# Context rows of V from DRAM, GpSimd interleaving and running sums in a chunked-attention and feed-forward kernel

## The chip, the cores and the metric

One core of a Trainium2 chip runs the whole program. The metric is device microseconds of one execution. TensorE is called PE in the profile, VectorE DVE, ScalarE ACT, GpSimd POOL and SyncE SP. The last two also issue DMAs: GpSimd those that convert float32 to float16 on the way (loads of q, k, v and the weights), SyncE all others, the DMA transposes among them.

## The reference, cut to what matters

```python
# q, k, v: (4, 8, 768, 64); mem_k, mem_v: (4, 8, 8, 64)
chunk, left_ctx, right_ctx = (32, 16, 8)
for c in range(24):
    ...
    k_ctx = k[:, :, l_start:r_end]          # 16 before, the chunk, 8 after
    v_ctx = v[:, :, l_start:r_end]
    k_full = np.concatenate([mem_k, k_ctx], axis=2)
    v_full = np.concatenate([mem_v, v_ctx], axis=2)
    a = softmax(scale * q_c @ k_full.T)
    out[:, :, c_start:c_end] = a @ v_full
# heads side by side: x is (4, 768, 512)
mu, var = x.mean(-1), ((x - mu) ** 2).mean(-1)
xn = (x - mu) / np.sqrt(var + 1e-06) * g_ln
result = x + np.maximum(xn @ w_ch1, 0.0) @ w_ch2     # 512 -> 2048 -> 512
```

## The kernel before, in words

The 4 x 768 rows are 24 tiles of 128 rows, six to a batch. A tile holds four chunks, which are worked in two groups of two chunks, so a batch has 12 groups of 64 rows. A group has 96 columns of keys and 96 rows of values: 8 memory rows, 16 rows from the left, 64 of its own, 8 from the right. In `V` (two buffers, by batch) a group's values stand on 96 partitions: memory on 0 to 7, left context on 8 to 23, its own rows on 24 to 87, right context on 88 to 95. In `KT` (two buffers) the keys stand transposed, 96 columns for each group and pair of heads.

Attention of a tile is `scores` (16 small matmuls), two `soften` (exponentials on ScalarE), `values` (16 small matmuls; column 64 of each head gives the sum for the softmax), then a reciprocal and a multiplication on VectorE, which leave x in float32 in `xs`. `stats` gives mean and variance on VectorE, `norm` writes (x - mean) * g to `xn`, and `root` makes the reciprocal of the deviation on GpSimd (`veps`, `rstd`); it is applied at the very end, in `finish`. `turn_x` transposes xn to `xT`, by TensorE for the first six tiles and by a DMA transpose on SyncE's queue for the others.

The feed-forward part works on units of three tiles, eight units, `u` from 0 to 7. Each unit has 28 steps: 16 `up` steps (four matmuls of 384 columns, then a relu, on VectorE for even steps and on ScalarE for odd ones) and 12 `down` steps (four matmuls of 512 columns; the last of each tile is followed by `finish` on VectorE and a store). `up_tile` does one chunk of four hidden blocks for a single tile. PSUM gives the ups and downs four banks (`mm0` to `mm3`) and attention two double banks (`att`).

The order is written by hand: `at(u, step, ...)` puts a piece of other work behind a step, `attend` places a tile's attention in this way, and every engine does its share in the order of the program. Step s of unit u is written (u, s) here. Ahead of unit 0 stands a front, in which the first three tiles are worked while weights arrive; there, TensorE also does dummy matmuls (`warm`).

Keys and queries of batch 0 are turned by TensorE (`turn_tile`). For batches 1 to 3, `load_block` loads a block of 256 rows, in two DMAs; `mix` interleaves it on ScalarE from `st` into `iv`; `cross` transposes it by DMA on SyncE's queue into `rawk` (keys) or `QR` (queries); and `spread` copies `rawk` into `KT` in three copies on VectorE, with `key_left` and `key_right` for the context between tiles. `load_v` loads values. Its default covers a group's own 64 rows, and `v_left` and `v_right` then copy the context from neighbouring groups, between partitions, by DMAs on SyncE's queue (V<-V in the profile); for the first groups of batch 0 the loads already bring some context rows. `v_mem` copies the memory values into V.

## Time and profile before

| what | us |
|---|---|
| median of 3 runs (lowest, highest) | 292.23 (290.86, 293.84) |
| profiled execution, its own time | 292.26 |
| its span, first to last instruction | 290.5 |
| TensorE busy | 228.5 (79%) |
| VectorE, GpSimd, ScalarE busy | 148.4, 120.5, 87.6 |
| mean granted clock of TensorE | 0.894 of full speed |

The span is what the trace covers; the rest of an execution lies around it. Shares of busy time are means over stages with different limits.

### The profile page before, as it was taken

Reading aid. Unit: us, or ns where it says so; the run is one execution under the profiler, and the core shown is the slowest. Engines: PE = TensorE matmul, PEld = TensorE weight load, DVE = VectorE, ACT = ScalarE, POOL = GpSimd, SP = SyncE. Lnnn points to the kernel's source line nnn. Section 1 sums busy time; section 2 is a strip of 40 time slices with the busy share of each in tenths; the row PEclk is TensorE's granted clock in tenths of the full one; section 3 lists DMA queues with packets and bytes.
Section 4 is the critical chain, followed back from the end, with each engine's and each line's share of the span. In section 5 each row is a group of like instructions: output and inputs, shape, how many; then the busy total and the mean of one; then the engine's idle time right before and its main releaser. Section 6 shows DMA issues by size and latency. Waiting matters only on the chain.

```text
span 290.5 us, 5094 instructions
## 1 busy us (share of the span) xinstructions
PE 228.5 (79%) x2024; PEld 132.9 (46%) x2024; DVE 148.4 (51%) x306; ACT 87.6 (30%) x148; POOL 120.5 (41%) x173
## 2 busy tenths in 40 slices
PE   7575899747095859996092999999086999999994
PEld 3353654446072325652051555654043646645644
DVE  5475543825314653726563463737574853863412
ACT  2424224133244103732240321642123603510400
POOL 8872630499920218656900119474930130110000
PEclk9979799997777868999589699999658999999999
DMA  6999990288999345999964024999946122012012
GB/s 109 165 184 208 196 140 2 72 125 93 139 130 93 90 80 67 158 86 147 164 128 67 18 56 77 157 102 138 182 93 101 20 66 82 18 54 93 0 38 72
DMA packets 87096, 29.12 MB, mean 100 GB/s; under 512 B 74872, under 2 KB 83344, under 8 KB 87024
## 3 DMA queue, kind: packets, MB, share of 16 engines
q0 software_dynamic: 53632, 13.86, 50.9%
q1 hardware_dynamic: 33440, 14.94, 29.5%
q8 instruction: 16, 0.26, 0.4%
q14 instruction: 8, 0.07, 0.1%
HBM read 27.95 MB, written 6.29 MB: 118 GB/s over the span
## 4 chain that ended last, share of the span: by engine, by line
PE 48%; DMA 26%; DVE 9%; POOL 6%; issue 4%; SPq 3%; ACT 2%; DVEq 0%; ACTq 0%; POOLq 0%
PE mm L335 20%; PE mm L361 19%; DMA V<-V 7%; DMA rawk<-iv 5%; DMA QR<-iv 4%; DMA out_dram<-osb 3%; DVE KT L100 3%; DMA st<-in_q_dram 3%; PE att L251 2%; PE att L272 2%; POOL st L123 2%; DMA st<-in_k_dram 2%; SPq L228 2%; DMA xT<-xn 2%; POOL V L100 2%
## 5 line engine op out<-in xcount | busy, mean ns | idle before, releaser
L335 PE MATMUL mm<-xT,w1c 128*128 128x384 f16 (+1 forms) x496 | 93.6, 345 | 20.4 <-DMA xT<-xn 17.1
L361 PE MATMUL mm<-w2c,rT 128*128 128x512 f16 x368 | 88.2, 394 | 0.0
L335 PEld LDWEIGHTS <-w1c 128*128 128x128 f16 x496 | 56.0, 118 | 48.9 <-issue 29.7
L327 ACT ACTIVATE rT<-mm 128x384 f16<-128x384 f32 (+2 forms) x66 | 31.8, 484 | 109.6 <-DVE rT L329 51.7
L300 POOL TENSOR_SCALAR veps<-mv 128x1 f32<-128x1 f32 x24 | 10.1, 423 | 116.2 <-DVE mv L290 115.9
L329 DVE TENSOR_SCALAR rT<-mm 128x384 f16<-128x384 f32 (+2 forms) x65 | 35.3, 545 | 39.1 <-PE mm L335 36.1
L361 PEld LDWEIGHTS <-rT 128*128 128x128 f16 x368 | 35.5, 101 | 41.9 <-issue 5.3
L261 ACT ACTIVATE AT<-att,band 96x512 f16<-96x512 f32 x48 | 31.1, 679 | 23.9 <-PE att L251 23.7
L100 DVE COPY KT<-rawk 128x288 f16<-128x288 f16 (+2 forms) x27 | 22.7, 894 | 28.5 <-DMA rawk<-iv 28.5
L130 POOL DMA_DIRECT2D V<-in_v_dram x48 | 34.8, 730 | 5.0 <-DMA V<-in_v_dram 2.8
L370 DVE SCALAR_TENSOR_TENSOR osb<-mm,rstd,xs 128x512 f32<-128x512 f32 x23 | 17.0, 746 | 26.8 <-PE mm L361 25.2
L98 ACT COPY iv<-st 128x1024 f16<-128x1024 f16 x18 | 18.6, 1042 | 38.0 <-DMA rawk<-iv 22.3
L272 PE MATMUL att<-V,AT 96*64 96x65 f16 x384 | 11.9, 208 | 19.5 <-DMA V<-V 17.3
L272 PEld LDWEIGHTS <-AT 96*64 96x64 f16 x384 | 9.3, 119 | 27.4 <-issue 18.9
L100 POOL COPY V<-memv 8x2560 f16<-8x2560 f16 x9 | 21.5, 2413 | 0.0
L294 DVE SCALAR_TENSOR_TENSOR xn<-xs,mv,gb 128x512 f16<-128x512 f32 x24 | 17.9, 747 | 0.5
L279 DVE RECIPROCAL rec<-att 128x8 f32<-128x8 f32 x24 | 4.9, 203 | 24.1 <-PE att L272 24.0
L280 DVE TENSOR_TENSOR xs<-att,rec 128x512 f32<-128x512 f32 x24 | 16.6, 691 | 0.8
L289 DVE BATCH_NORM_STATS2 bst<-xs 128x6 f32<-128x512 f32 x24 | 16.6, 693 | 0.7
L346 PE MATMUL mm<-xT,w1c 128*128 128x128 f16 x112 | 10.0, 260 | 8.3 <-ACT rT L327 7.2
L251 PE MATMUL att<-QR,KT 64*96 64x64 f16 x384 | 14.2, 216 | 1.5 <-DVE KT L100 1.2
L251 PEld LDWEIGHTS <-KT 64*96 64x96 f16 x384 | 11.5, 129 | 8.3 <-issue 5.7
(55 smaller groups left out, 129.5 us busy)
## 6 DMA issues: line engine op xcount, KB each, us to landing
out_dram<-osb SPq DMA_DIRECT2D x23, 256.0 KB, 2.7
st<-in_k_dram POOLq DMA_DIRECT2D x24, 128.0 KB, 7.4
st<-in_q_dram POOLq DMA_DIRECT2D x24, 128.0 KB, 8.1
V<-in_v_dram POOLq DMA_DIRECT2D x40, 64.0 KB, 8.3
w1c<-in_moe_w_ch_dram POOLq DMA_DIRECT2D x4, 512.0 KB, 8.9
w2c<-in_moe_w_ch_dram POOLq DMA_DIRECT2D x4, 512.0 KB, 10.5
V<-in_v_dram POOLq DMA_DIRECT2D x5, 88.0 KB, 7.9
V<-V SPq DMA_DIRECT2D x2, 220.0 KB
```

The lines of the kernel that those rows point to most:

```text
L98: eng.copy(out=out, in_=in_)
L100: eng.tensor_copy(out=out, in_=in_)
L130: nc.gpsimd.dma_start(out=V[b % 2][lo:hi, g, :, 0:64], in_=dram(v, b * H * HS + (64 * g - 24 + lo) * D, [[64, hi - lo], [HS, H], [1, 64]]),)
L251: nc.tensor.matmul(out=p[0:W, par, (4 * gg + j) * 64 : (4 * gg + j) * 64 + 64], lhsT=KT[b % 2][rows, t, j, gg, :], rhs=free(QR[b % 2][rows ...
L261: nc.scalar.activation(out=free(AT[t % 3], 32 * c, [[64, 16], [1, 32]]), in_=free(p, 4 * c, [[64, 16], [1, 4], [8, 8]], W), func=ACTF.Exp, ...
L272: nc.tensor.matmul(out=p[64 * gg : 64 * gg + 64, par, HD * j : HD * j + HD], lhsT=AT[t % 3][:, par, gg, j, :], rhs=V[b % 2][:, 2 * t + gg, ...
L294: nc.vector.scalar_tensor_tensor(out=xn[i % 4], in0=xs[i % 9], scalar=mv[t][:, 0:1], in1=gb, op0=ALU.subtract, op1=ALU.mult,)
L327: nc.scalar.activation(out=o, in_=p, func=ACTF.Relu)
L329: nc.vector.tensor_scalar(out=o, in0=p, scalar1=0.0, scalar2=None, op0=ALU.max)
L335: nc.tensor.matmul(out=p, lhsT=free(w1c[c][:, dt, :], i, [[4, 128]]), rhs=xT[u % 2][:, dt, 128 * lo : 128 * (lo + n)], start=(dt == 0), st ...
L361: nc.tensor.matmul(out=p, lhsT=rT[c][:, k_, 128 * i : 128 * i + 128], rhs=w2c[c][:, k_, :], start=(c == 0 and k_ == 0), stop=(c == 3 and k ...
L370: nc.vector.scalar_tensor_tensor(out=o, in0=p, scalar=rstd[t % 9], in1=xs[t % 9], op0=ALU.mult, op1=ALU.add,)
```

## The change

- `load_v` now loads each group's context rows from DRAM as well (88 rows; 72 and 80 at a batch's ends), for all batches. `v_left` and `v_right` are gone.
- `mix` runs on GpSimd, and `iv` has four buffers instead of two. The loads, mixes and memory copies of a batch are one list, `ahead`; the transposes (`cross`) of a batch are placed at fixed steps.
- In `spread`, two of the three copies go to ScalarE. `KT` is laid out by group.
- `root` of all tiles of a unit stands in that unit's own steps 3 to 5 (12 for one tile, 16 to 18 in unit 0), not behind the tile's attention.
- The sum over x comes from the multiplication that writes it (`accum_out`), the mean is that sum times -1/512 (`nmean`), and the sum of squared deviations (`sq`) is a Square on ScalarE with its accumulator.
- In the front, the loads, the attention of three tiles and six `up_tile` are ordered anew; unit 0 starts at up step 8 instead of 4. The load of g is issued later.

```diff
-    def load_v(b, g, lo=24, hi=88):
+    def load_v(b, g):
+        lo, hi = 24 if g == 0 else 8, 88 if g == NG - 1 else 96
...
-    def v_left(b, g0, g1):
...
-    def spread(b, blk, eng):
+    def spread(b, blk, eng, e1):
-        copy(eng, free(kt, 768 * t + 24, [[192, 4], [8, 9], [1, 8]]),
+        copy(e1, free(kt, 768 * t + 24, [[96, 4], [8, 9], [1, 8]]),
...
-        nc.vector.tensor_tensor(
-            out=x.rearrange("p (a h d) -> p a h d", a=2, h=4),
...
+        nc.vector.scalar_tensor_tensor(
+            out=x.rearrange("p (h d) -> p h d", h=8),
+            in0=free(p, 0, [[128, 8], [1, 64]]), scalar=1.0,
+            in1=free(r, 0, [[1, 8], [0, 64]]),
+            op0=ALU.mult, op1=ALU.mult, accum_out=tot[t],
+        )
+        nc.vector.tensor_scalar(
+            out=nmean[t], in0=tot[t], scalar1=-1.0 / 512, scalar2=None, op0=ALU.mult
+        )
...
-        nc.vector.bn_stats(out=bst[t % 3], in_=x)
-        nc.vector.bn_aggr(out=mv[t], in_=bst[t % 3])
+        nc.scalar.activation(
+            out=junk, in_=xs[(NT * b + t) % 9], func=ACTF.Square, bias=nmean[t], scale=1.0,
+            accum_out=sq[t],
+        )
...
-        at(u, s1 + 2, root, b, t)
-        at(u, s1 + 3, turn_x, b, t)
+        at(u, s1 + 1, norm, b, t)
+        at(u, s1 + 2, turn_x, b, t)
+        at(u, s1 + 2, stats, b, t)
+        at(i // 3, 12 if i == 5 else 3 + i % 3, root, b, t)
...
+        order = [(load_pair, (0,)), (load_pair, (1,))]
+        order += [(mem_cols, (pool,)), (v_mem, (0, 4, pool)), (mix_pair, (0,))]
+        order += [(load_v, (g,)) for g in range(3)]
+        order += [(mix_pair, (1,)), (v_mem, (4, 8, pool))]
...
+            ahead(1, order, 23, 0.3)
+            for blk, s in ((0, 1), (1, 4), (2, 14)):
...
+                at(1, s + 4, spread, 1, blk, dve, act)
+            attend(6, 11, 14, 1)
+            attend(7, 14, 18, 1)
+            attend(8, 18, 22, 1)
...
+            ahead(b, order, U * (u - 1), 1)
+            for blk, s in ((0, 7), (1, 12), (2, 24)):
```

GpSimd's queue behind the last loads of batch 0, in the kernel before (a name's number tells buffers apart; `st` and `V` are loads of batch 1, `mv` the statistics of a tile):

```order
L300 TENSOR_SCALAR veps_133<-mv_130 128x1
L304 TENSOR_TENSOR rstd_139<-veps_133,mhalf 128x1
L300 TENSOR_SCALAR veps_134<-mv_131 128x1
L304 TENSOR_TENSOR rstd_140<-veps_134,mhalf 128x1
L123 DMA st_87<-in_k_dram 128x1x512 x2
L123 DMA st_88<-in_q_dram 128x1x512 x2
L100 COPY KT_96<-memKT 128x24x8 x2
L100 COPY V_94<-memv_67 8x2560
L123 DMA st_81<-in_k_dram 128x1x512 x2
```

The same place in the changed kernel, from the root of the front's last tile on:

```order
L296 TENSOR_SCALAR veps_147<-sq_140 128x1
L300 TENSOR_TENSOR rstd_150<-veps_147,mhalf 128x1
L125 DMA st_87<-in_k_dram 128x1x512 x2
L125 DMA st_88<-in_q_dram 128x1x512 x2
L125 DMA st_81<-in_k_dram 128x1x512 x2
L125 DMA st_82<-in_q_dram 128x1x512 x2
L102 COPY KT_98<-memKT 128x48x8
L102 COPY V_96<-memv_67 8x2560
L102 COPY iv_89<-st_87 128x2x8x64
L102 COPY iv_90<-st_88 128x2x8x64
L133 DMA V_96<-in_v_dram 72x8x64
```

The roots of tiles 3 and 4 no longer stand ahead of the loads of batch 1, and the interleaves (`iv`) now stand in this queue.

SyncE's queue from the last output of unit 0 on, before:

```order
L373 DMA out_dram<-osb_123 128x512
L137 DMA V_93<-V_93 16x1280
L141 DMA V_93<-V_93 8x640
L228 DMA_TRANSPOSE rawk_91<-iv_89 128x8x128
L228 DMA_TRANSPOSE QR_98<-iv_90 128x8x128
L228 DMA_TRANSPOSE rawk_92<-iv_89 128x8x128
L228 DMA_TRANSPOSE QR_98<-iv_90 128x8x128
L137 DMA V_94<-V_94 16x3200
L141 DMA V_94<-V_94 8x3200
```

And now:

```order
L369 DMA out_dram<-osb_125 128x512
L221 DMA_TRANSPOSE rawk_93<-iv_89 128x8x128
L221 DMA_TRANSPOSE QR_100<-iv_90 128x8x128
L221 DMA_TRANSPOSE rawk_94<-iv_91 128x8x128
L221 DMA_TRANSPOSE QR_100<-iv_92 128x8x128
L221 DMA_TRANSPOSE rawk_93<-iv_89 128x8x128
L221 DMA_TRANSPOSE QR_100<-iv_90 128x8x128
L308 DMA_TRANSPOSE xT_117<-xn_115 128x4x128
```

The copies between partitions are gone, and the transposes of batch 1 follow one another, each from a buffer of its own up to the fourth.

VectorE in the first steps of unit 1, from the values of tile 5 on, before:

```order
L279 RECIPROCAL rec_146<-att_147 128x8
L280 TENSOR_TENSOR xs_107<-att_147,rec_146 128x512
L289 BN_STATS bst_126<-xs_107 128x6
L290 BN_AGGR mv_132<-bst_126 128x2
L329 TENSOR_SCALAR rT_119<-mm_152 128x256
L294 SCALAR_TENSOR_TENSOR xn_112<-xs_107,mv_132,gb 128x512
L322 COPY xT_116<-att_148 128x4x128
L329 TENSOR_SCALAR rT_119<-mm_150 128x256
L329 TENSOR_SCALAR rT_120<-mm_152 128x256
L329 TENSOR_SCALAR rT_117<-mm_149 128x4x128
L100 COPY KT_96<-rawk_91 128x4x72
```

And now:

```order
L272 RECIPROCAL rec_158<-att_160 128x8
L273 SCALAR_TENSOR_TENSOR xs_109,tot_131<-att_159,rec_158 128x512
L279 TENSOR_SCALAR nmean_137<-tot_131 128x1
L102 COPY KT_98<-rawk_93 128x8x88
L325 TENSOR_SCALAR rT_120<-mm_161 128x256
L285 SCALAR_TENSOR_TENSOR xn_114<-xs_109,nmean_137,gb 128x512
L318 COPY xT_118<-att_159 128x4x128
L325 TENSOR_SCALAR rT_121<-mm_163 128x256
```

The first spread copy of batch 1 moved up, ahead of the norm of tile 5.

## Rows read from the trace of the kernel before

**Rows 1.** The page: busy time of each engine, share of the span, instructions.

```profile
PE 228.5 (79%) x2024; PEld 132.9 (46%) x2024; DVE 148.4 (51%) x306; ACT 87.6 (30%) x148; POOL 120.5 (41%) x173
```

**Rows 2.** Waits of TensorE (PE), whole span: total us, times, longest us.

```profile
PE att L272 <- DMA V<-V: 17.3, 5, 4.8
PE mm L335 <- DMA xT<-xn: 17.1, 2, 9.3
...
PE mm L346 <- ACT rT L327: 7.2, 1, 7.2
```

**Rows 3.** Timeline of TensorE: start, us, instruction, idle time before it.

```profile
31.19 4.51 PE L335 MATMUL mm<-xT,w1c 128*128 128x384 f16 x24
36.91 4.06 PE L335 MATMUL mm<-xT,w1c 128*128 128x384 f16 x24 [1.21 <-DVE rT L329]
40.81 1.03 PE L361 MATMUL mm<-w2c,rT 128*128 128x512 f16 x4
...
57.88 1.47 PE L335 MATMUL mm<-xT,w1c 128*128 128x256 f16 x12 [0.22 <-DVE xT L322]
...
71.69 1.06 PE L346 MATMUL mm<-xT,w1c 128*128 128x128 f16 x16
...
127.79 7.94 PE L361 MATMUL mm<-w2c,rT 128*128 128x512 f16 x36
```

**Rows 4.** Windows: us, busy PE, PEld, DVE, ACT, POOL; clock, DMA share, GB/s.

```profile
80.40:100.90 20.50, 17.58 (x169) 10.45 (x168) 8.48 (x19) 7.33 (x12) 3.00 (x6) 0.76 0.97 106
111.60:135.70 24.10, 24.10 (x209) 13.58 (x207) 14.28 (x28) 10.41 (x17) 14.68 (x24) 1.00 1.60 117
265.80:290.50 24.70, 20.99 (x129) 13.39 (x127) 7.59 (x13) 3.93 (x8) 0.00 (x0) 1.00 0.12 43
```

**Rows 5.** Timeline of GpSimd (POOL): first loads of batch 1; copies of batch 2.

```profile
38.49 0.55 POOL L304 TENSOR_TENSOR rstd<-veps,mhalf 128x1 f32<-128x1 f32 x1
...
55.61 0.19 POOL L300 TENSOR_SCALAR veps<-mv 128x1 f32<-128x1 f32 x1 [3.15 <-DVE mv L290]
...
56.37 1.59 POOL L123 DMA_DIRECT2D st<-in_k_dram  x2
...
138.58 7.01 POOL L100 COPY V<-memv 8x2560 f16<-8x2560 f16 x3
```

**Rows 6.** Groups by line and form: count, busy us, mean ns, idle before.

```profile
L289 DVE BATCH_NORM_STATS2 bst<-xs 128x6 f32<-128x512 f32 x24 | 16.6, 693 | 0.7
...
L290 DVE BATCH_NORM_AGGREGATE mv<-bst 128x2 f32<-128x6 f32 x24 | 4.4, 182 | 0.8
...
L294 DVE SCALAR_TENSOR_TENSOR xn<-xs,mv,gb 128x512 f16<-128x512 f32 x24 | 17.9, 747 | 0.5
...
L100 POOL COPY V<-memv 8x2560 f16<-8x2560 f16 x9 | 21.5, 2413 | 0.0
...
L100 POOL COPY KT<-memKT 128x192 f16<-128x192 f16 x6 | 1.9, 352 | 0.0
...
L98 ACT COPY iv<-st 128x1024 f16<-128x1024 f16 x18 | 18.6, 1042 | 38.0 <-DMA rawk<-iv 22.3 <-DMA QR<-iv 13.8 <-DMA st<-in_k_dram 2.0
```

**Rows 7.** DMA queue in 175:205: packets, MB, share of 16 engines.

```profile
q0 software_dynamic: 11087, 2.18, 93.5%
```

**Rows 8.** Timeline of SyncE (SP): two key transposes of batch 1.

```profile
69.55 1.34 SPq L228 DMA_TRANSPOSE rawk<-iv  x1
...
77.07 2.37 SPq L228 DMA_TRANSPOSE rawk<-iv  x1
```

**Rows 9.** Timeline of VectorE (DVE): spread copies that waited for transposes.

```profile
75.92 1.50 DVE L100 COPY KT<-rawk 128x288 f16<-128x288 f16 x3 [2.38 <-DMA rawk<-iv]
...
86.90 1.41 DVE L100 COPY KT<-rawk 128x288 f16<-128x288 f16 x3 [2.02 <-DMA rawk<-iv]
...
141.07 5.52 DVE L100 COPY KT<-rawk 128x288 f16<-128x288 f16 x3 [5.81 <-DMA rawk<-iv]
```

**Rows 10.** DMA issues, whole span: count, median us to landing.

```profile
rawk<-iv SPq DMA_TRANSPOSE x9, 3.1
```

More of the change, by code (lines that the diff above doesn't have):

```diff
@@ L447 @@
     nc.vector.memset(V[0][64:96, NG - 1, :, :], 0.0)
[L448 to L449 removed]
     load_tile(0, 1, 1)
+    load_v(0, 0)
+    load_v(0, 1)
     load_tile(0, 2, 0)
     load_w1(0)
[L453 to L454 removed]
+    load_v(0, 2)
+    load_v(0, 3)
     load_tile(0, 2, 1)
     load_tile(0, 3, 0)
[L457 to L460 removed]
+    load_w1(1)
+    load_v(0, 4)
+    load_v(0, 5)
+    load_w1(2)
+    load_w1(3)
     load_w2(0)
@@ L470 @@
     load_v(0, 8)
-    load_v(0, 9, 24, 96)
+    load_v(0, 9)
     load_w2(3)
@@ L493 @@
     soften(0, 0, 1)
-    turn_tile(0, 1, 1, dve, dve)
-    ones(0, 2, NG)
-    count_v(0, 1, NG - 1)
-    warm(3)
-    turn_tile(0, 2, 0, dve, act)
-    v_mem(0, 0, 2, dve)
-    values(0, 0)
-    stats(0, 0)
-    norm(0, 0)
+    turn_tile(0, 1, 1, dve, dve, mm[2])
+    warm(1)
+    turn_tile(0, 2, 0, dve, act, mm[0])
+    warm(1)
     scores(0, 1)
@@ L505 @@
     soften(0, 1, 1)
-    warm(4)
+    values(0, 0)
+    norm(0, 0)
+    warm(2)
+    turn_tile(0, 2, 1, dve, act, mm[2])
     turn_x(0, 0)
     warm(2)
-    v_mem(0, 2, 6, dve)
     values(0, 1)
+    norm(0, 1)
+    turn_tile(0, 3, 0, dve, act, mm[1])
     up_tile(0, 0, 0, act)
-    stats(0, 1)
-    norm(0, 1)
-    turn_tile(0, 2, 1, dve, act)
-    turn_tile(0, 3, 0, dve, act)
     scores(0, 2)
@@ L521 @@
     values(0, 2)
-    stats(0, 2)
     norm(0, 2)
+    up_tile(0, 1, 0, act)
+    up_tile(0, 1, 1, dve)
+    turn_x(0, 2)
+    up_tile(0, 0, 2, act)
+    up_tile(0, 1, 2, dve)
+    for t in range(3):
+        stats(0, t)
     for b in range(1, B):
         mem_vals(b)
-    warm(3)
-    turn_x(0, 2)
-    up_tile(0, 0, 2, act)
-    for t in range(3):
-        root(0, t)
     def early(i):
@@ L565, in block @@
             at(u, s1 + 5, spread, b, blk, dve)
-    at(0, 4, v_mem, 0, 6, NG, dve)
-    at(0, 5, early, 1)
-    at(0, 15, v_left, 0, 6, 8)
-    at(0, 15, v_right, 0, 6, 7)
+    for t in range(3):
+        at(0, 16 + t, root, 0, t)
+    at(0, 9, v_mem, 0, 6, NG, dve)
+    at(0, 12, early, 1)
     turns(0, 4, 0, 0, 16)
@@ L577 @@
     attend(4, 22, 24, 0)
-    at(0, 22, v_left, 0, 8, 10)
-    at(0, 22, v_right, 0, 8, 9)
-    turns(0, 5, 1, 0, 27)
-    at(1, 0, v_left, 0, 10, 12)
-    at(1, 0, v_right, 0, 10, 11)
-    attend(5, 2, 6, 1)
-    U = 28
-    def later(b, order, u0):
-        for fn, args, s in order:
-            at(u0 + s // U, s % U, fn, *args)
-    def batch(b, off, gap, vgap, groups):
-        order = []
-        s = off
-        for blks, gs in groups:
-            for blk in blks:
-                for which in range(2):
-                    order.append((load_block, (b, blk, which), s))
-                    m = s + 8
-                    order.append((mix, (b, blk, which, act), m))
-                    order.append((cross, (b, blk, which), m + 1))
-                    if which == 0:
-                        order.append((spread, (b, blk, dve), m + 6))
-                    s += gap
-            for g in gs:
-                order.append((load_v, (b, g), s))
-                s += vgap
-        return order
@@ L610, with ahead, load_pair @@
-    order = batch(1, 27, 1, 1, (((0, 1), range(6)), ((2,), range(6, 12))))
-    later(1, order, 0)
-    for b in (2, 3):
-        order = batch(b, 0, 2, 1, [((i,), range(4 * i, 4 * i + 4)) for i in range(3)])
-        later(b, order, 2 * b - 2)
+    turns(0, 5, 1, 0, 25)
+    attend(5, 1, 5, 1)
+    U = 28
+    def ahead(b, order, s, gap):
+        for fn, args in order:
+            at(int(s) // U, int(s) % U, fn, *((b,) + args))
+            s += gap
+    def load_pair(b, blk):
+        load_block(b, blk, 0)
+        load_block(b, blk, 1)
```

142 lines of the change are left out of this document (66 added, 76 removed).

## The prediction

> **What bounds the kernel now.** I read the page's busy line first, then the list of waits, then TensorE's timeline, then the windows. TensorE is busy for 228.5 us of 290.5, so 62 us are idle [rows 1]. Three waits hold two thirds of that [rows 2]: 17.3 us in five waits until the copies of V between partitions (V<-V) have landed, 17.1 us in two waits until transposed xn have landed in xT, and 7.2 us behind a relu on ScalarE. In the timeline [rows 3] unit 1 starts at 57.88, and the windows [rows 4] show unit 2 from 111.6: 53.7 us for unit 1. Unit 2 waits for nothing and takes 24.1 us; unit 7 with the last stores takes 24.7. So the loss lies in unit 1 and at the starts and inside of units 3 and 5; in the others TensorE itself is the bound, and a faster engine there brings nothing.
>
> Why unit 1 is late is read on GpSimd's queue [rows 5]: it is free at 39.04, then stands before the roots of tiles 3 and 4, which need statistics that VectorE has yet to make (the second starts at 55.61), and issues the first load of batch 1 at 56.37. Everything of batch 1 (loads, interleave, transpose, spread, V<-V) follows from there.
>
> **The change, part by part.** All sums are made on the profiled execution: 292.26 us, of which 290.5 is the span; 1.8 us lie around it. The median of the runs is 292.23, so no correction is needed.
>
> *Front.* The three normalisations lose a BN_STATS and a BN_AGGR each, 0.69 + 0.18 us [rows 6], ahead of xn, which TensorE waits for; the added nmean on a 128x1 tile is bounded by zero and by the 0.18 of that aggregate. Three more chunk tiles of w1 (16 matmuls, 1.06 us [rows 3]) fill places where dummy matmuls stood. The q load of tile 2 keeps its place in GpSimd's queue and now stands ahead of the first transpose of xn, so the start gains nothing and the gains come behind it; the later load of g is covered by the same wait (uncovered, about 1 us, an estimate). I put the first full-width up step at 29.5 instead of 31.19 (31.2 if the arriving weights set it, 28 if only VectorE does). From there 8 steps remain instead of 12, at 4.06 / 6 = 0.68 us each [rows 3], 5.4 us, and 0.5 of the wait behind the clearing of V that stays between two relus. The downs start at 35.4 instead of 40.81.
>
> *Downs of unit 0.* They took 40.81 to 57.88, 17.1 us [rows 3]. The transposes of xn there lose 0.88 us of statistics. 16.2 remain, so unit 1 starts at 51.6.
>
> *Unit 1 without waits.* 16 steps of 256 columns at 1.47 / 3 = 0.49 us, 4 chunk tiles at 1.06, 12 downs at 7.94 / 9 = 0.88 [rows 3], and four tiles of attention at about 0.9 (an estimate: 32 small matmuls each): 7.8 + 4.2 + 10.6 + 3.5 = 26.1 us, to 77.7.
>
> *Loads of batch 1.* The roots stand behind them now, so GpSimd can issue the first at about 39 instead of 56.4 [rows 5]. V<-V is gone, with all its waits. In its place V has 1032 rows a batch instead of 768, in 8 heads: 2112 more runs of 128 bytes. The software queue's 11087 packets took 93.5% of 16 engines' 30 us, 40 ns each [rows 7], so this adds 5.3 us of DMA time per batch, beside TensorE's work.
>
> *Interleave on GpSimd.* It leaves ScalarE, 18 x 1.04 us, and with it the queue in which it stood before relus. On GpSimd no row has it. Its copies took 2.41 us for 2560 elements and 0.35 for 192 [rows 6]: 0.94 to 1.8 ns per element, so 0.96 to 1.9 us for 1024; I take 1.08, on the line between the two. What is queued behind each: V loads of later groups, and who waits for those: values, steps later. 18 of them bring GpSimd from 120.5 [rows 1] to 140 us busy, well under any span considered here.
>
> *Squares on ScalarE, two of three spread copies on ScalarE.* The nearest row for a square of 512 is ScalarE's interleave of 1024, 1.04 us [rows 6]; 24 squares at no more than that replace 18 interleaves, and ScalarE is busy 10.4 of the 24.1 us of unit 2 [rows 4]. Nothing on the path; the cover is the pair of relu engines, each needed every other step. But the spread now holds both relu engines while its transpose has not landed.
>
> *What is late next: the transposes.* SyncE's queue holds nothing else between the third output of unit 0 and the transposes of blocks 0 and 1, and by the sum above their interleaves are done at about 50 and 54, so all four go out from 52 on. Their price is in the rows: issued at 69.55, the first key transpose let VectorE go on at 75.92; issued at 77.07, the second let it go on at 86.90 [rows 8, 9]. That is 6.4 to 9.8 us while loads run; loads run in the new kernel too (39 to about 75). Taking them in a row at 4 to 5 us each gives keys 0 at 57, queries 0 at 61, keys 1 at 65, queries 1 at 69. The spread of block 0 stands at step 5 of unit 1, 54.5, ahead of norm(5) and of the next relus: VectorE waits 2.5 us. Scores(6) at step 11 and the spread of block 1 at step 8 come at about 57 to 60 and wait until 61 and 65. Then relus are free at 66 to 67 instead of 57 for the step at which TensorE runs out of free banks. I charge 10 us (2 if the transposes take 3 us each, 19, nearly what the waits of unit 1 were, if they take 10). After a wait of 7.2 us the granted clock of 80.4 to 100.9 was 0.76, a mix of 2.4 and 1.2 GHz, 4.9 us lost in 20.5 [rows 4]; I charge 3. Tile 8's chain from values at step 22 (reciprocal, scaling, nmean, a finish and the norm on VectorE, the largest 0.75 [rows 6], some 2.5 in all; then an output and a transpose on SyncE, some 4) is 6.5 us, an estimate, and five downs cover 4.4 of it: 2 us. Unit 2 starts at 77.7 + 15 = 92.7.
>
> *Units 2 to 7.* Batch 2 is loaded from about 75 and batch 3 from about 115, ahead of use, so units 3 to 6, which have unit 2's steps, take its 24.1: 5 x 24.1 + 24.7 = 145.2, to 237.9. In place of the 17.1 us before units 3 and 5 [rows 2], I keep 2 us each: the same seven transposes (four large, three of xn) took about 25 us in unit 2 and now start with the unit instead of 8 us into it. End of the span 241.9, with 1.8 around it **243.7 us**, on record as 243.
>
> **A rule against the change.** While GpSimd copied memory values into V, from 138.58 to 145.59 [rows 5], three spread copies of VectorE took 5.52 us instead of 1.50 [rows 9]. The Trainium skill (GPSIMD Engine Reference, section 1, Specifications) says that GpSimd shares its SBUF interfaces with VectorE and contends with VectorE's two-port modes and its instructions with two SBUF inputs. By that rule, the trace agrees, at least for the first kind. It is a rival below.
>
> **Rivals.**
> Hidden transposes: loads come 17 us sooner, and if the DMA engines have gaps between V loads the transposes land in about 3 us, as the one did whose landing ended a wait that could be timed, 3.1 [rows 10]. Against it: the software queue fills the engines while loads run [rows 7]. Then of the 15 us in unit 1 remain 2, and of the 4 later about 2: 228 us.
> Transposes bind in every batch: V's extra runs and the same contention leave 19 us in unit 1 and the 17.1 us before units 3 and 5: 243 + 9 + 13 = 265 us. For it: it is the same queue and the same seven transposes. Against it: only two interleave buffers and late loads held them back before, now four.
> VectorE held by GpSimd: 18 interleaves and 9 copies into V meet 9 large spread copies and 24 norms. If each spread loses one 2.41 us copy on the path, 9 x 2.41 = 22 us, less the 4 charged before units 3 and 5, which lie in the same steps: 261 us. Against it: only one copy per spread is left on VectorE, and most spreads lie beside downs, which need no relu.
> Slower than before: GpSimd's one queue becomes the bound. Interleaves wait there for landings, and roots for ScalarE, with V loads behind. If a batch takes P us on it, block 1 of batch 3 is ready at about 39 + 2.55 P, and 83 us of TensorE's work follow (12 downs, units 5 to 7). This passes 295 from P = 68 on. Busy time alone gives at most 140 / 3 = 47, so some 21 us of waits a batch would be needed; at P = 70 it is 303 us.
>
> **How the numbers follow.** Forecast 0.52 (own range 234 to 253), hidden 0.24, transposes bind 0.12, VectorE held 0.08, slower 0.04. The range runs from 227, the hidden case, to 262, which takes in the held case and leaves out the upper end of the binding one and the slower one. A measurement of this kernel tells about 1% from no change. All cases but the last are faster by far more; some chance is kept for no change, if two of the bad cases meet: 0.94, 0.02, 0.04.
>
> **What the profile after would show.** No V<-V; first load of batch 1 near 39 to 42; first key spread of batch 1 waiting for rawk with relus of both engines behind it; unit 1 starting near 52 and unit 2 near 93; idle of TensorE near 15 to 20 us behind 50; VectorE without BN and GpSimd near 140 us busy. The prediction is wrong if unit 2 starts before 82 (transposes hidden), if interleaves on GpSimd take over 2 us, or if a wait of TensorE on values or scores remains in units 3 to 6.

## The result and the profile after

The changed kernel takes **265.25 us** (median of 4 runs, 263.43 to 268.94) where the kernel before took 291.55 beside it (288.33 to 293.84): a ratio of 0.911, 95% interval 0.900 to 0.923. It is faster, by less than forecast: 243 was on record, with a range from 227 to 262. A ratio compares only executions within 1.5% of the fastest of the same kernel, so it can differ from the quotient of two medians. The profiled execution is one of 263.43 us with a span of 261.7.

The page's busy line, which answers to [rows 1]:

```profile
PE 220.0 (84%) x2048; PEld 132.2 (51%) x2048; DVE 122.3 (47%) x288; ACT 97.6 (37%) x195; POOL 142.7 (55%) x188
```

TensorE's idle time has gone from 62 to 41.7 us. The list of TensorE's waits over the whole span, in total us, times and longest us, answers to [rows 2]:

```profile
PE mm L331 <- DMA xT<-xn: 11.7, 3, 9.2
PE att L313 <- DVE xn L285: 9.9, 2, 9.2
PE mm L342 <- ACT rT L323: 3.8, 1, 3.8
PE mm L194 <- DMA st<-in_q_dram: 3.5, 1, 3.5
PE mm L194 <- DMA st<-in_k_dram: 2.5, 2, 2.2
PE mm L342 <- ACT KT L100: 2.4, 1, 2.4
```

The waits for V<-V are gone. A wait for xn on VectorE has come, and two waits in the front for copies and loads. Their places are in TensorE's timeline, which answers to [rows 3]: start, us, instruction, and in brackets the idle time before it with what ended it.

```profile
19.85 0.63 PE L194 MATMUL mm<-identity,st 64*64 64x64 f16 x16 [3.52 <-DMA st<-in_q_dram]
...
25.45 1.86 PE L342 MATMUL mm<-xT,w1c 128*128 128x128 f16 x16 [2.43 <-ACT KT L100]
...
37.00 3.41 PE L331 MATMUL mm<-xT,w1c 128*128 128x384 f16 x20
...
43.23 1.03 PE L357 MATMUL mm<-w2c,rT 128*128 128x512 f16 x4
...
59.58 1.04 PE L331 MATMUL mm<-xT,w1c 128*128 128x256 f16 x8
...
73.57 0.61 PE L313 MATMUL att<-identity,xn 128*128 128x128 f16 x4 [9.24 <-DVE xn L285]
82.26 1.86 PE L342 MATMUL mm<-xT,w1c 128*128 128x128 f16 x16 [3.75 <-ACT rT L323]
136.63 4.03 PE L331 MATMUL mm<-xT,w1c 128*128 128x384 f16 x12 [9.18 <-DMA xT<-xn]
189.29 2.12 PE L331 MATMUL mm<-xT,w1c 128*128 128x384 f16 x12 [1.89 <-DMA xT<-xn]
```

Four things are to be seen. The front is later than before, not earlier: full-width up steps from 37.00 instead of 31.19, downs from 43.23 instead of 40.81. Unit 1 starts at 59.58, 1.7 us later than before. Unit 1 still loses 13 us in two waits. And 9.18 us stand ahead of unit 3.

What these waits hang on is read on SyncE and VectorE. On SyncE's timeline, transposes of keys at the start of unit 1 (they answer to [rows 8]) and in unit 2:

```profile
61.06 2.84 SPq L221 DMA_TRANSPOSE rawk<-iv  x1
...
65.60 5.30 SPq L221 DMA_TRANSPOSE rawk<-iv  x1
...
112.36 2.58 SPq L221 DMA_TRANSPOSE rawk<-iv  x1
```

On VectorE's timeline, the spread copies that read them (these answer to [rows 9]) and the norm behind the last one:

```profile
71.72 0.81 DVE L102 COPY KT<-rawk 128x704 f16<-128x704 f16 x1 [7.22 <-DMA rawk<-iv]
...
80.60 1.05 DVE L102 COPY KT<-rawk 128x704 f16<-128x704 f16 x1 [5.10 <-DMA rawk<-iv]
...
127.37 0.81 DVE L102 COPY KT<-rawk 128x704 f16<-128x704 f16 x1 [10.25 <-DMA rawk<-iv]
...
130.82 0.74 DVE L285 SCALAR_TENSOR_TENSOR xn<-xs,nmean,gb 128x512 f16<-128x512 f32 x1
```

From issue to use, the three transposes take 10.7, 15.0 and 15.0 us. While VectorE stands at the third, tile 11's chain stands behind it; its xn is made at 130.82, its transpose is issued at 131.63, and unit 3, which needs it, starts at 136.63. The DMA issues of 85 to 135 (count of issues, median us to landing) show the same for xn and for keys. In the list of [rows 10], over the whole span of before, the medians were 2.5 for xn, 3.1 for keys and 8.9 for queries:

```profile
xT<-xn SPq DMA_TRANSPOSE x6, 10.7
rawk<-iv SPq DMA_TRANSPOSE x3, 7.7
QR<-iv SPq DMA_TRANSPOSE x2, 4.6
```

### The profile page after: what moved, and what is told of

Same layout as the page of the kernel before. It is cut to its first block, busy times and chain, and to the rows that moved or that the text cites. A ratio compares the mean times of both kernels' runs of the same rounds, so it can differ in the third digit from the quotient of the medians.

```text
span 261.7 us, 5110 instructions
## 1 busy us (share of the span) xinstructions
PE 220.0 (84%) x2048; PEld 132.2 (51%) x2048; DVE 122.3 (47%) x288; ACT 97.6 (37%) x195; POOL 142.7 (55%) x188
## 3 DMA queue, kind: packets, MB, share of 16 engines
q0 software_dynamic: 72320, 14.84, 65.9%
## 4 chain that ended last, share of the span: by engine, by line
PE 47%; DMA 26%; POOL 18%; issue 4%; DVE 2%; ACT 2%; POOLq 0%; ACTq 0%; DVEq 0%
DMA st<-in_q_dram 22%; PE mm L331 19%; PE mm L357 18%; POOL V L133 7%; POOL st L125 4%; DMA rawk<-iv 3%; PE mm L342 3%; POOL iv L102 3%; PE att L244 2%; PE att L265 2%; POOL rstd L300 1%; PE mm L379 1%; DMA xT<-xn 1%; POOL V L102 1%; POOL st L117 1%
## 5 line engine op out<-in xcount | busy, mean ns | idle before, releaser
L331 PE MATMUL mm<-xT,w1c 128*128 128x384 f16 (+1 forms) x480 | 86.3, 333 | 12.7 <-DMA xT<-xn 11.7
L331 PEld LDWEIGHTS <-w1c 128*128 128x128 f16 x480 | 53.1, 117 | 36.8 <-DMA xT<-xn 10.8
L323 ACT ACTIVATE rT<-mm 128x384 f16<-128x384 f32 (+2 forms) x65 | 31.2, 483 | 59.9 <-PE mm L331 28.1
L133 POOL DMA_DIRECT2D V<-in_v_dram x48 | 44.3, 929 | 1.9 <-DMA st<-in_k_dram 1.0
L254 ACT ACTIVATE AT<-att,band 96x512 f16<-96x512 f32 x48 | 31.2, 678 | 7.4 <-PE att L244 7.3
L100 ACT COPY KT<-rawk 128x288 f16<-128x288 f16 (+1 forms) x18 | 12.2, 726 | 45.6 <-DMA rawk<-iv 45.6
L366 DVE SCALAR_TENSOR_TENSOR osb<-mm,rstd,xs 128x512 f32<-128x512 f32 x23 | 17.1, 749 | 24.3 <-PE mm L357 18.6
L102 POOL COPY iv<-st 128x1024 f16<-128x1024 f16 x18 | 19.0, 1074 | 16.4 <-DMA st<-in_q_dram 8.5
L290 ACT ACTIVATE junk<-xs,nmean 128x512 f16<-128x512 f32 x24 | 17.2, 716 | 15.0 <-DVE nmean L279 10.9
L102 DVE COPY KT<-rawk 128x704 f16<-128x704 f16 x9 | 8.4, 936 | 30.6 <-DMA rawk<-iv 30.6
L285 DVE SCALAR_TENSOR_TENSOR xn<-xs,nmean,gb 128x512 f16<-128x512 f32 x24 | 19.9, 829 | 0.4
L342 PEld LDWEIGHTS <-w1c 128*128 128x128 f16 x160 | 13.4, 129 | 8.4 <-issue 8.0
L273 DVE SCALAR_TENSOR_TENSOR xs<-att,rec 128x512 f32<-128x512 f32 x24 | 16.6, 692 | 0.8
L300 POOL TENSOR_TENSOR rstd<-veps,mhalf 128x1 f32<-128x1 f32 x24 | 13.9, 579 | 2.0
```

The source lines that it names most:

```text
L102: eng.tensor_copy(out=out, in_=in_)
L133: nc.gpsimd.dma_start(out=V[b % 2][lo:hi, g, :, 0:64], in_=dram(v, b * H * HS + (64 * g - 24 + lo) * D, [[64, hi - lo], [HS, H], [1, 64]]),)
L254: nc.scalar.activation(out=free(AT[t % 3], 32 * c, [[64, 16], [1, 32]]), in_=free(p, 4 * c, [[64, 16], [1, 4], [8, 8]], W), func=ACTF.Exp, ...
L285: nc.vector.scalar_tensor_tensor(out=xn[i % 4], in0=xs[i % 9], scalar=nmean[t], in1=gb, op0=ALU.add, op1=ALU.mult,)
L290: nc.scalar.activation(out=junk, in_=xs[(NT * b + t) % 9], func=ACTF.Square, bias=nmean[t], scale=1.0, accum_out=sq[t],)
L323: nc.scalar.activation(out=o, in_=p, func=ACTF.Relu)
```

## The experiments

Each kernel is compared with the kernel before, run beside it (medians 292.7, 295.3, 293.2 and 293.0 in the four sets), and with 265.25 of the changed kernel. The changed kernel was not run again in these sets, and the kernel before differs by up to 3.7 us between its medians; a difference of that size between kernels of two sets is not told apart here.

**The order of SyncE's queue in unit 1.** cross_early puts the transposes of batch 1's blocks 0 and 1 ahead of the last outputs of unit 0, and starts its loads 3 steps earlier in the program.

```diff
-            ahead(1, order, 23, 0.3)
+            ahead(1, order, 20, 0.3)
-                    if blk:
+                    if blk == 2:
                         at(1, s, cross, 1, blk, which)
                     else:
-                        at(0, 27, cross, 1, 0, which)
+                        at(0, (21, 24)[blk], cross, 1, blk, which)
```

> The changed kernel, with the four transposes of blocks 0 and 1 of batch 1 placed ahead of the three outputs of unit 0 in SyncE's queue (same order on GpSimd). Theory A (SyncE's queue order holds them back: their interleaves were done at 53 and 58, the first went out at 61.1): the first key transpose goes out near 52, the wait of TensorE for norm(5), 9.2 us, falls below 3 us, unit 2 starts near 95 instead of 103, the kernel is 6 to 9 us faster than the changed one, about 257 us. Rival B (the DMA engines are full from 45 to 85 whatever the order): transposes that go out earlier land as much later, unit 2 starts at 101 to 103, about 264 us.

259.32 us (254.04, 255.90, 262.74 and 267.96), ratio 0.872 (0.863 to 0.881). The rows are from the execution of 254.04. The loads of batch 1 start where they did (42.23 instead of 42.58). The transposes go out at 51.50 to 57.83 instead of 61.06 to 70.99, and the wait of 9.24 us for xn is 1.90. But TensorE's timeline then has a new wait ahead of unit 2, for the transposed xn of tile 8, issued at 84.80, and keeps most of the one ahead of unit 3:

```profile
65.81 0.40 PE L313 MATMUL att<-identity,xn 128*128 128x128 f16 x4 [1.90 <-DVE xn L285]
95.43 2.75 PE L331 MATMUL mm<-xT,w1c 128*128 128x384 f16 x8 [8.79 <-DMA xT<-xn]
127.68 4.03 PE L331 MATMUL mm<-xT,w1c 128*128 128x384 f16 x12 [6.57 <-DMA xT<-xn]
```

From the start of unit 1 to that of unit 2 it is 36.27 us instead of 43.65, the new wait included, so the place in the queue did hold unit 1. Part of the gain was given back behind it.

**The place of the spreads.** spread_late moves block 1's spread of batches 2 and 3 from step 16 to step 21; spread2_late moves block 2's too, from step 0 of the next unit to its step 21 (the last line of the diff, which spread_late doesn't have).

```diff
-                if s + 4 < U:
+                if blk == 1:
+                    at(u - 1, 21, spread, b, blk, dve, act)
+                elif s + 4 < U:
                     at(u - 1, s + 4, spread, b, blk, dve, act)
                 else:
-                    at(u, 0, spread, b, blk, dve, act)
+                    at(u, 21, spread, b, blk, dve, act)
```

> The changed kernel, with the spread of block 1 of batches 2 and 3 at step 21 of its unit instead of 16, behind the norm of the unit's last attention tile. Theory A (VectorE stood 10.3 us before that spread, ahead of values(11), and so made xn for unit 3 late): xn(11) is done near 121.5 instead of 131.5, the wait of 9.2 us before unit 3 falls to 1 to 3 us, and with the clock that is then kept the kernel is 8 to 10 us faster, about 256 us. Rival B (xT's transposes are themselves slow behind the loads, 11 us to landing): xn(11) is early, but xT lands at 131 to 134, the wait falls by 3 to 5 us only, about 261 us.

> For batches 2 and 3 the key spreads of block 1 and of block 2 both stand later in the program: block 1 at step 21 of the unit ahead instead of step 16, block 2 at step 21 of the unit that first needs block 1's keys instead of step 0. The theory: with one spread moved (spread_late) the 9.18 us wait ahead of unit 3 went, but a wait of 7.12 us for a relu stood in unit 3, since the spread of block 2 was then the one that stood in VectorE's and ScalarE's queue with its transpose 12 us under way. With both moved, both waits go, and the ones like them ahead of unit 5 too: 251 to 255 us, against 265 of the changed kernel. The rival: the transposes of xn, which share SyncE's queue with those of the keys, come as late, and the wait moves to xT at the start of units 3 and 5: a gain of 3 us at most, 262 to 266. A third way: block 2's keys are now too late for the scores of tile 3 at step 1 of the next unit, and those hold TensorE by 2 to 4 us.

spread_late: 266.59 us (264.85 to 268.29), no gain. The wait ahead of unit 3 fell from 9.18 to 0.54 as expected, and 11 us on there was one that had not been there:

```profile
130.69 2.14 PE L331 MATMUL mm<-xT,w1c 128*128 128x384 f16 x12 [0.54 <-DMA xT<-xn]
141.85 3.68 PE L331 MATMUL mm<-xT,w1c 128*128 128x384 f16 x11 [7.12 <-ACT rT L323]
```

In ScalarE's timeline of the same kernel, the relu that TensorE waited for stands behind the spread of block 2, whose transpose had been issued at 128.01:

```profile
140.05 1.36 ACT L100 COPY KT<-rawk 128x288 f16<-128x288 f16 x2 [13.70 <-DMA rawk<-iv]
```

spread2_late: 257.16 us (252.99 to 258.93). Between 120 and 180 us no wait over 0.3 us is left; 3.71 ahead of unit 2 and 2.28 ahead of unit 5 stay. The time is 2 us above the range expected. So the 9.18 us were the spread's place, as far as a step order can show it, and moving one of two spreads only changed which one held the relus. The third way in the expectation, scores that wait for late keys, did not come.

**What makes the transposes slow.** v64 loads only 64 rows of each group of V in batches 2 and 3 (the context rows of these batches are left out); no_v loads no V in them; no_loads loads nothing at all in them, so that they work on what batches 0 and 1 left in the buffers. The diff is that of no_loads; no_v has its second part alone, and v64 has `lo, hi = 24, 88` there in place of the return.

```diff
     def load_block(b, blk, which):
         s = pick(st, ("b", b, blk, which))
+        if b > 1:
+            return
...
     def load_v(b, g):
         lo, hi = 24 if g == 0 else 8, 88 if g == NG - 1 else 96
+        if b > 1:
+            return
```

> The changed kernel, with only 64 rows a group loaded for V of batches 2 and 3: the context rows of these two batches are left out and keep older values. Theory A (V's extra runs slow the transposes of units 2 and 4 as they fill the DMA engines): the key transpose of block 1 of batch 2 takes 10 us instead of 15 to landing, the wait before unit 3 falls from 9.2 to about 4, the kernel is 4 to 6 us faster, about 260 us. Rival B (the transposes are slow beside any loads): the landing stays at 13 to 15 us, the kernel is within 2 us of 265.

> Leaves out all loads of V in batches 2 and 3, so that these batches work with the values of batches 0 and 1; all else stands as in the changed kernel. The theory that GpSimd's loads slow the transposes of SyncE's queue: the transposes of keys and of xn in units 2 to 5 land in 3 to 5 us instead of 10 to 15, and the waits of 9.2 us ahead of unit 3 and 1.9 ahead of unit 5 vanish: 248 to 254 us. The rival: the transposes wait on each other (eight lie in SyncE's queue at a time) or on the loads of queries and keys, which stay: they still take over 8 us, and the time falls by less than 3 us, to 262 to 265.

> Leaves out every load of batches 2 and 3 (values, keys and queries), so that these batches work on what batch 1 and batch 0 left in the buffers; mixes, transposes, spreads and all else stand where the changed kernel has them. Without the values alone, GpSimd came to the next batch's loads of keys and queries sooner, and these took their place: a transpose of keys issued at 126.78 landed 15.3 us later. The theory that any loads of GpSimd's queue slow the transposes: now those of units 2 to 5 land in 3 to 5 us, and no wait over 2 us stands ahead of units 3 and 5 or in them: 250 to 255 us (the front and unit 1 keep their loads and their waits). The rival, that the transposes on SyncE's queue slow each other or the outputs do: they still take over 7 us, the waits stay, 262 to 266.

v64 264.16, no_v 265.12 (ratio 0.916, 0.903 to 0.930), no_loads **248.97** (248.25 to 249.67; 0.858, 0.850 to 0.866). Leaving out rows of V, or all of V, changes nothing that is measured in the time. In no_v the key transpose of block 2, issued at 126.78, was used at 142.06: without V, GpSimd sent the next batch's keys and queries at 124.20 to 129.57, and it took 15.3 us beside these. With no loads at all the landings in 100 to 130 are:

```profile
xT<-xn SPq DMA_TRANSPOSE x4, 2.4
rawk<-iv SPq DMA_TRANSPOSE x3, 3.3
QR<-iv SPq DMA_TRANSPOSE x3, 3.7
```

Over the same 85 to 135 as above, the four kernels are, in us:

| kernel | GpSimd's queue, share of 16 engines | median xn, keys, queries | time |
|---|---|---|---|
| changed | 89.5% | 10.7, 7.7, 4.6 | 265.25 |
| v64 | 76.8% | 9.4, 9.2, 9.7 | 264.16 |
| no_v | 52.5% | 7.0, 5.1, 7.1 | 265.12 |
| no_loads | 9.1% | 2.4, 3.3, 3.7 | 248.97 |

The same transposes, in the same order on the same queue, beside the same outputs, land in 2.4 to 3.7 us instead of 4.6 to 10.7. So they do not slow each other to this extent; the loads do. Those of keys and queries are enough for it (no_v), and V's add to most of the medians; V's loads alone were not tried. TensorE's longest waits in that kernel are those of the front and of unit 1, whose loads it keeps:

```profile
PE att L317 <- DVE xn L289: 9.1, 3, 8.3
PE mm L346 <- ACT rT L327: 3.7, 1, 3.7
PE mm L198 <- DMA st<-in_k_dram: 3.1, 1, 3.1
PE mm L346 <- ACT KT L100: 2.4, 1, 2.4
```

The Trainium skill (DMA: Bandwidth & Descriptors, Queues, rings and completion order) says that each DMA engine goes round between its queues packet by packet. The trace agrees so far as a transpose of xn beside GpSimd's queue at 89.5% takes longer, 10.7 us instead of 2.4, and still lands; no run here shows the turns themselves.

**The front.** gb_early issues the load of g first on SyncE, as before the change. bank lets the transposes of tile 3's keys write to mm[0] instead of mm[1]. gb_bank does both.

```diff
+    nc.sync.dma_start(out=gb, in_=dram(moe_g_ln, 0, [[0, 128], [1, 512]]))
     PAIR = 1.0 / 128 + 15.0 / 2**20
...
-    nc.vector.memset(gb[:, 0:1], 0.0)
-    nc.sync.dma_start(out=gb, in_=dram(moe_g_ln, 0, [[0, 128], [1, 512]]))
...
-    turn_tile(0, 3, 0, dve, act, mm[1])
+    turn_tile(0, 3, 0, dve, act, mm[0])
```

> The changed kernel, with the load of g issued at the start as in the kernel before. Theory A (this load, issued at 7.6 into a full queue, took the DMA engines from the loads of w1 and q): the first chunk of w1 lands at 14.5 to 15.5 instead of 17.9, the q load of tile 2 at about 17.5 instead of 19.85, the downs of unit 0 start near 41 instead of 43.2, and the kernel is about 2 us faster, 263 us. Rival B (something else in the order of the loads): the q load still lands at 19.5 to 20 and the time is the same.

> The changed kernel with one thing changed in the front: the transposes of tile 3's keys write to another PSUM tile, mm[0] instead of mm[1], so that the first chunk tile of w1 (at 25.45 in the changed kernel, after 2.43 us of waiting) doesn't wait until VectorE has copied those keys out, which stands behind norm(0, 1). The theory that this wait and the low clock behind it (0.50 in 20 to 31) are the larger part of the 7.8 us by which the downs start later than forecast: they start at 39 to 40.5 instead of 43.23, and the time, if nothing behind gives it back, is 262 us. The rival: the arrival of tile 2's queries and of w1's first part sets the start, the wait is then for w1, and the downs start at 42 or later.

> Both front changes on the changed kernel: g loaded first, and tile 3's keys in mm[0]. No other step is moved. The theory that best's earlier downs (37.73) come from these two alone: the downs start at 37.5 to 38.5. What the 5 us are worth at the end is open: 260 if unit 1 and the transposes stand as they are, behind loads issued at the same time; 263 to 266 if the loads of batch 1, which hang on the roots and on GpSimd's queue and not on the front, set unit 1 whatever the front does.

In the changed kernel these keys leave the bank behind norm(0, 1), a part by VectorE and the rest by ScalarE, and the chunk tile of 25.45 starts when they are out:

```profile
24.33 0.55 DVE L102 COPY KT<-mm 128x32 f16<-128x32 f16 x2
24.97 0.43 ACT L100 COPY KT<-mm 128x320 f16<-128x320 f16 x1 [3.86 <-DVE KT L102]
```

gb_early 267.86 (261.9 to 270.61), not told apart from the changed kernel. In its profiled execution (269.17) the downs do start at 40.55, as expected, but 11.38 us are lost in unit 3 to a relu behind a spread on ScalarE that waited 18.09 us for its key transpose. bank **256.12** (253.63 to 257.91), ratio 0.878 (0.872 to 0.884). gb_bank 251.47 (251.18 to 254.98), ratio 0.859 (0.854 to 0.865). Both are faster than any value expected of them. The downs start at 37.90 with the bank alone and at 37.50 with both: the bank is worth 5.3 us of the front, and beside it the load of g 0.4. In bank's timeline of TensorE:

```profile
21.86 1.89 PE L342 MATMUL mm<-xT,w1c 128*128 128x128 f16 x16
37.90 1.03 PE L357 MATMUL mm<-w2c,rT 128*128 128x512 f16 x4
95.42 2.75 PE L331 MATMUL mm<-xT,w1c 128*128 128x384 f16 x8 [7.86 <-DMA xT<-xn]
```

The other profiles bear the bank out. In the changed kernel and the seven others with its front (v64, no_v, no_loads, cross_early, spread_late, spread2_late, mix_act) the downs start at 42.11 to 43.49, and in the four with the other bank at 37.12 to 37.90. The load of g is less certain: tile 2's queries are turned at 17.84 to 19.85 in the nine kernels that issue it late and at 17.40 to 18.61 in the four that issue it first, 0.9 us apart on the mean. The windows of the front (us, busy PE, PEld, DVE, ACT, POOL; clock, DMA share, GB/s), first of the changed kernel:

```profile
20.00:31.00 11.00, 8.06 (x108) 6.45 (x108) 3.21 (x10) 2.87 (x5) 4.93 (x8) 0.50 1.30 203
```

and of bank:

```profile
20.00:31.00 11.00, 9.56 (x159) 7.98 (x158) 6.55 (x18) 2.70 (x7) 4.31 (x7) 0.82 1.28 204
```

In 11 us the one issues 108 matmuls and the other 159. Of the 5.3 us, the wait in the rows above is 2.4, and tile 2's queries came 1.1 earlier in this execution (18.75 against 19.85); the 1.8 that remain fit the clock, which stands at 0.50 (1.2 GHz) in the whole window with that wait and at 0.82 without it: from the first chunk tile to the first full-width up step TensorE is busy for 10.8 us in the one and 8.8 in the other with the same matmuls. The clock was low before the wait already (16 transposing matmuls of 64 columns take 0.64 us at 12.81 and 0.63 at 19.85, and 0.44 at 9.83); with the wait it rises later. The rival, that w1's arrival sets the start, falls: the first chunk tile runs at 21.86 in bank and has its weights. At the end of the kernel the bank gave 9.1 us, 3.8 more than in the front, and I had not expected that. In the profiles unit 1 is 2.4 us shorter (41.22 from 54.20 to 95.42, the new wait of 7.86 for xn included) and the way from there to unit 3 is 2.7 shorter. The first key transpose of batch 1 is now issued at 55.67 and used at 61.36, 5.7 us instead of 10.7, and the wait of 9.24 us in unit 1 is 4.27. The loads of batch 1 hardly moved (40.90 instead of 42.58), so the transposes run beside an earlier part of them. That this is why they are faster agrees with no_loads, but no run tried it alone. Nor is it known why gb_bank, with a front only 0.4 us earlier, ends 4.7 us below bank.

**Parts of the change.** roots_only is the kernel before with the roots late; roots_v is that with values loaded with their context rows and no V<-V; mix_act is the changed kernel with the interleave on ScalarE again. The diff shows the line of the roots, which the first two share, and the main lines of mix_act.

```diff
-        at(u, s1 + 2, root, b, t)
+        at(i // 3, 12 if i == 5 else 3 + i % 3, root, b, t)
...
+                at(u - 1, s, mix, b, blk, 0, act)
+                at(u - 1, s, mix, b, blk, 1, act)
                 at(u - 1, s, cross, b, blk, 0)
```

> The kernel before with one part of the change: the two operations of the norm's root stand late in GpSimd's queue, at steps 3 to 5 of the unit that uses them (step 12 for tile 5), and nothing else is changed; values are still loaded without context rows and copied between partitions by SyncE, mixes are still on ScalarE. The theory that GpSimd's queue stood behind the roots: batch 1's loads are issued at about 39 to 42 us instead of 56, the transposes of its keys come some 10 us earlier, the 10 to 17 us that unit 1 and the start of unit 2 wait shrink, and the time is 280 to 286 us. The rival: mixes on ScalarE and the copies between partitions hold unit 1 and its successors whatever GpSimd does, and the time stays within 1% of 292.

> The kernel before with two parts of the change: the roots late (as in roots_only, 278.5 us), and values loaded with their context rows, so that SyncE's queue has no copies between partitions; mixes stay on ScalarE, statistics and front as before. roots_only's TensorE waits 8.8 us for those copies, and batch 1's key transposes stand behind them in SyncE's queue. The theory that both parts add up: 266 to 270 us, so that these two parts alone give the whole gain of the change, and the rest of it (mixes on GpSimd, running sums, the front) gives nothing that is measured. The rival, that the wait moves to the transposes of xn and to those of keys, which stay on the same queue: 274 to 279.

> The changed kernel with one part undone: the interleaving copies of batches 1 to 3 are on ScalarE again, right ahead of the transposes that read them, instead of on GpSimd between the loads. Adds 18 copies of about 1.04 us to ScalarE (97.6 us busy) and takes them from GpSimd. The theory that GpSimd's place for them was not what held the kernel: GpSimd's loads go out earlier still, the transposes are no faster, and the time is 262 to 270. The rival, that mixes between GpSimd's loads hold up the keys or that GpSimd's copies slow VectorE's norms (0.83 against 0.75 us): 255 to 260.

roots_only 278.54 (ratio 0.964, 0.948 to 0.981), roots_v 276.03 (0.951, 0.944 to 0.958), mix_act 274.28 (0.944, 0.935 to 0.954). By the ratios, 3.6% of the change's 8.9% is one line, GpSimd no longer standing before statistics (the interval is 1.9 to 5.2%). Values with context rows add little that is told apart, 2.5 us between kernels of two sets: 8.8 us of waits for V<-V go, and the wait ahead of unit 3 grows from 9.32 to 10.20 and that ahead of unit 5 from 4.90 to 7.12, so the rival was right. Putting the interleave back on ScalarE costs 9.0 us, and here my own expectation (262 to 270) was wrong. ScalarE has time for it, 113.9 us busy, and none of the 18 interleaves there waits for its load. What TensorE waits for in mix_act is a norm in unit 1 (10.23 us, 9.24 in the changed kernel) and then relus, 5.17 and 3.58 us ahead of the downs of units 2 and 4 and 9.58 in unit 3, while the waits of 9.18 and 1.89 ahead of units 3 and 5 are gone. The relus stand behind spreads that wait for key transposes, as in spread_late; in ScalarE's timeline, ahead of that of 9.58:

```profile
145.38 1.36 ACT L100 COPY KT<-rawk 128x288 f16<-128x288 f16 x2 [15.41 <-DMA rawk<-iv]
```

Why this comes out 9 us dearer than the same transposes in the changed kernel was not taken apart. The rest of the change, front and running sums, has about 2 us left to explain (mix_act against roots_v), which the runs do not tell from nothing.

**All together.** best is the changed kernel with the front, the order of SyncE's queue and both late spreads; best_hold also holds GpSimd's loads of batches 2 and 3 back behind the roots of tiles 8 and 14.

```diff
-        at(i // 3, 12 if i == 5 else 3 + i % 3, root, b, t)
+        at(i // 3, 12 if i == 5 else 0 if i in (6, 7, 8, 12, 13, 14) else 3 + i % 3, root, b, t)
```

> The changed kernel with all the moves that helped one by one: the load of the norm's weights first in SyncE's queue (front some 2 us earlier); the transposes of tile 3 of batch 0 in another bank, so that the first up tile doesn't wait for their evacuation (2.4 us); batch 1's key transposes ahead of the outputs in SyncE's queue (unit 1, 6 us); and the late spreads of blocks 1 and 2 (9 us ahead of unit 3). The theory that each removes a wait of its own: 240 to 250 us. The rival, that each wait removed exposes the next one on the transposes of xn: 254 to 260, no better than cross_early's 259.

> The kernel best (251.4 us) with one more step: GpSimd does the roots of tiles 6 to 8 ahead of batch 2's loads, and those of tiles 12 to 14 ahead of batch 3's, and so waits for the statistics of tiles 8 and 14 before it issues these loads (in best they were issued from 77.83 and 123.01). In best TensorE waits 8.12 us ahead of unit 2, 3.69 ahead of unit 3 and 3.49 ahead of unit 5 for the transposes of xn, which are then on their way beside these loads and take up to 8.6 us. The theory that the loads slow the transposes: the waits ahead of units 2 and 4 or 5 fall by 3 to 5 us, and the time is 245 to 249. The rival: later loads bring the keys of these batches later, and the time stays within 1% of 251 or grows.

best 251.37 (249.28 to 252.79), ratio 0.869 (0.855 to 0.884); best_hold **246.98** (243.35 to 249.42), ratio 0.843 (0.830 to 0.857). best is just above the 240 to 250 expected and no faster than gb_bank: once the front is early, the moves in SyncE's queue and of the spreads give nothing more, since TensorE waits for the transposes of xn as long as in gb_bank (15.3 and 15.5 us in three waits). Holding the loads back, which is what no_loads points to, brings another 4 us; the intervals overlap by a little, so this step is likely rather than certain. In the profile of best_hold the wait of 8.12 us ahead of unit 2 is gone, as expected, while those ahead of units 3 and 5 grew from 3.69 and 3.49 to 5.81 and 4.77. Both beat the two kernels compared.

## Why the prediction was wrong

The span was forecast at 241.9 and is 261.7. Read off the timeline against the sums on record, the 19.8 us are: the start of unit 1 +8.0 (59.58 against 51.6), unit 1 +2.5 (43.65 us to unit 2 at 103.23, against 41.1), units 2 to 7 +9.3, of which +7.3 up to the start of unit 3 at 136.63, +2.5 inside unit 3 and -0.5 behind. The windows of units 2 and 3 answer to [rows 4]:

```profile
103.23:127.45 24.22, 24.22 (x208) 13.66 (x208) 9.41 (x21) 10.14 (x21) 16.64 (x16) 1.00 1.51 101
136.60:163.20 26.60, 26.48 (x208) 14.65 (x209) 12.03 (x28) 10.87 (x22) 14.71 (x20) 0.90 1.03 107
```

**Front: the step that failed first.** "The downs start at 35.4": 43.23. I counted what statistics and dummies left, and bounded the first full-width up step by 28 and 31.2; it came at 37.00. What was not in the sum is that the new order puts tile 3's key transposes in the bank that the first chunk tile writes, with their copies out of it on VectorE behind norm(0, 1) and on ScalarE behind that: 2.4 us of waiting, and a clock that stays at 0.50. With another bank the step comes at 31.66 and the downs at 37.90. Of the 2.5 us that remain the load of g is 0.4 (0.9 by the means above), though the sum took it as covered; the others were not taken apart, and in bank a wait of 4.51 us for tile 2's queries, to 18.75, stands ahead of them. With that one bank the whole kernel takes 256.12, inside the range.

**Waits ahead of units 3 and 5: a term mis-sized.** "I keep 2 us each": 9.18 and 1.89. The mechanism was on record, transposes taken at 6.4 to 9.8 us while loads run, but for unit 1 I reckoned with 4 to 5 each in a row, and for these waits with a start early enough to hide them. They took 15 where it mattered, and the spread that stood ahead of tile 11's norm passed that on whole; spread2_late and no_loads show the two halves of it. Unit 3 then loses 2.5 us to the clock, 0.90 against 1.00 in unit 2; I had charged the clock in unit 1 alone.

**Unit 1: right in kind, and near in the sum by some luck.** 15 us were charged beyond the work itself: 10 for waits behind the transposes, 3 for the clock, 2 ahead of unit 2. 17.5 came: 13.0, 3.9 (TensorE busy for 29.98 us where 26.1 were reckoned, at a clock of 0.80) and 0.7. The 4.9 us that the sum gave as lost to the clock in the window of before counted its idle time too: TensorE was busy there for 17.58 of 20.5 us, so that 4.2 is the most. The kind was named, a spread that waits for rawk and holds norm(5) and relus. The split was not: the first wait was put at 2.5 us on VectorE and took 7.22 there and 9.24 of TensorE's time, since the first key transpose took 10.7 us and not 5, and the later wait was the shorter one, 3.75.

**What came as forecast.** GpSimd 142.7 us busy (140); the first load of batch 1 at 42.58 (39 to 42), right behind the front's last root; no V<-V; no wait for values or scores from unit 2 on. The interleave on GpSimd, which no row of before had, took what the line between its two copies gave, 1.08:

```profile
L102 POOL COPY iv<-st 128x1024 f16<-128x1024 f16 x18 | 19.0, 1074 | 16.4 <-DMA st<-in_q_dram 8.5 <-issue 4.3 <-DMA st<-in_k_dram 3.5
```

**The rivals.** "Transposes bind in every batch" gave 265, the measured time, but by another sum: it kept the 17.1 us ahead of units 3 and 5 and all of the forecast's front, while 11.1 came there and 8 in the front; that the two agree is chance. "Hidden transposes" is refuted by the landings above. "VectorE held by GpSimd" would have a spread lose 2.4 us. The nine spread copies on VectorE take 0.77 to 1.29 us, 8.4 in all, and 7.3 in mix_act, so what is lost there is near 1 us and not 22. The norms, which read two tensors, lose as little: 20 of the 24 take 0.74 or 0.75 us, and four take 1.08 to 1.42, all four while GpSimd copies (three beside an interleave, one beside a copy into V). The mean is 829 ns, and 754 in mix_act, where ScalarE interleaves: 1.8 us over 24 norms. The Trainium skill (GPSIMD Engine Reference, section 1, Specifications) says that GpSimd contends with instructions of VectorE that have two SBUF inputs. The trace agrees, by these four norms. In VectorE's groups of the changed kernel, and then of mix_act:

```profile
L285 DVE SCALAR_TENSOR_TENSOR xn<-xs,nmean,gb 128x512 f16<-128x512 f32 x24 | 19.9, 829 | 0.4
```

```profile
L285 DVE SCALAR_TENSOR_TENSOR xn<-xs,nmean,gb 128x512 f16<-128x512 f32 x24 | 18.1, 754 | 0.4
```

**What stays open.** Why the front's 5.3 us grew to 9.1 at the end is argued from where the transposes fall among the loads, and not shown by a run of its own. Nor was it tried whether bank and held-back loads alone, without best's other moves, reach best_hold's time.

## What to carry to other kernels

When loads are brought forward, price everything else that uses the DMA engines by its duration beside loads, not by its duration alone, and hold the loads back by a real dependency where a short transfer is on the path. An instruction that waits for a transfer belongs behind whatever else its in-order engine must deliver, and of several such instructions all have to move, or the next one takes the wait over. When code is reordered, list for each PSUM buffer who must empty it and what stands ahead of that on its engine: one bank number was worth 9 us here.
